# Turning the attention output of step 3 by transposing DMAs from SyncE in place of TensorE

## The chip, the cores and the metric

The kernel runs on one core of a Trainium2 chip. The metric is the time on the device in microseconds (us), lower is better. Executions of the kernel before on one chip agree here within about 1%. A granted TensorE clock of 1.00 is full speed: FFN matmuls of 384 columns then come every 0.163 us (kernel before, 16 of them from 50.08, clock 1.00 in the stretch 50 to 60).

## The reference, cut to what matters

```python
# attention, 4 batches x 8 heads x 768 positions x 64; five heads keep only 4 sink columns and a window of 64
scores = where(mask, q @ k.T / sqrt(64), -1e9)
a = softmax(scores)
attn = a @ v                                   # (B, H, S, D)
# FFN on the attention output, heads side by side: x is (3072, 512)
x = attn.transpose(0, 2, 1, 3).reshape(B * S, H * D)
h = max(x @ w1, x @ w2, x @ w3)                # (3072, 768)
out = h @ w_out                                # (3072, 512)
```

The kernel's FFN matmuls take x with its 512 features on the partitions (the tiles xT below), so each piece of attention output is turned first.

## The kernel before: the parts that matter

Work is cut into 16 steps t: four batches, two halves of 384 rows each, and in each half two quads of four heads. A step has two head pairs i, and each gives one tile x of 128 rows by 3 blocks of 128 columns. Two steps make the four tiles xT (hp = 0 to 3) that one half's FFN needs. Steps 0, 1 and 3 turn x on TensorE with a copy out of PSUM; the others do it by a transposing DMA from SyncE's queue:

```python
BY_DMA = (2, 4, 5, 6, 7, 8, 9, 10, 11, 12, 13, 14, 15)

def av(t, i):
    # ... value products into a PSUM bank o ...
    nc.vector.reciprocal(out=rc, in_=o[:, :, :, D])
    x = xp.tile([P, HB, 2, D], FP16, tag="x", name="x")
    nc.vector.tensor_tensor(out=x, in0=o[:, :, :, 0:D], in1=rc..., op=ALU.mult)     # cut
    if t in BY_DMA:
        nc.sync.dma_start(
            out=xT[b, half][hp], in_=x.rearrange("p a h d -> p (a h d)"), transpose=True
        )
    else:
        xs[t, i] = x

def turn_x(t, i, op=None):
    if t not in BY_DMA:
        # ... three TensorE transposes into tr, then one copy tr -> xT (VectorE for step 3) ...
    if hp == NHP - 1:
        queue.append(ffn(b, half))          # from here on this half's FFN is interleaved
```

The FFN's first product accumulates over the four tiles in turn, so the two tiles of step 3 are its third and fourth matmul:

```python
for ks in range(KS):
    nc.tensor.matmul(yy[:, 0:HALF], w_t[wi][:, ks, ...], xT[b, half][ks]..., start=(ks == 0), stop=(ks == KS - 1))
```

The softmax here doesn't subtract the row's maximum and nothing guards it: scores larger than these inputs give would overflow.

## Time and profile before

| | before |
|---|---|
| time, median | 200.65 us (200.58 to 200.71) |
| TensorE busy | 189.7 of 199.3 us, 95% |
| TensorE waits after 50.2 us | none |

In the list of waits a line reads: who waited on whose result, microseconds in total, how often, the longest. The kernel before:

```profile
PE tr L527 <- DVE x L505: 1.2, 3, 0.6
PE st L441 <- DVE KQ L190: 0.8, 2, 0.5
```

The first is the wait of the x transposes for VectorE, of which 0.64 us belongs to step 3. The second is that of step 4's scores for the turned keys, 0.53 us, directly behind step 3's transposes.

### The profile page before, as it was taken

To read this page: it belongs to the slowest core of one execution; us is meant where nothing else is said; L and a number is where in the kernel's file an instruction comes from. 1 tells how busy PE (TensorE), PEld (TensorE's weight loads), DVE (VectorE), ACT (ScalarE), POOL (GpSimd) and SP (SyncE) were. 2 spreads that over 40 slices of the span, in tenths; PEclk is the share of its full clock that TensorE was granted. 3 is DMA by queue.
4 is the path that set the end of the run, shared out by engine and by line. 5 is a ranking of instruction groups with operands and counts; after the bars stand their busy time and mean duration, and the time that the engine had idled before them with its cause. 6 is when DMAs were issued, how large, how long until landed. Compare 5 with 4: busy or idle time off the path is not lost.

```text
span 199.3 us, 5133 instructions
## 1 busy us (share of the span) xinstructions
PE 189.7 (95%) x2059; PEld 109.5 (55%) x2059; DVE 122.5 (61%) x241; ACT 131.7 (66%) x206; POOL 123.3 (62%) x154
## 2 busy tenths in 40 slices
PE   7897999996999999999999999999999999999992
PEld 2455555545566465574555565565555565755652
DVE  2698587999687829861555649961555234543540
ACT  4585798786966776676786775848758769323221
POOL 3599159789887906787969635799847447400000
PEclk9999999999999999999999999999999999999999
DMA  6999999994949991904359995513410250023004
GB/s 182 270 213 245 278 238 212 213 202 112 256 81 154 194 274 43 178 0 146 95 101 132 170 254 141 85 26 98 116 23 20 105 76 20 3 64 135 3 0 158
DMA packets 43245, 26.48 MB, mean 133 GB/s; under 512 B 33558, under 2 KB 38230, under 8 KB 43222
## 3 DMA queue, kind: packets, MB, share of 16 engines
q1 hardware_dynamic: 37206, 15.01, 34.9%
q0 software_dynamic: 4784, 10.23, 26.7%
q10 hardware_dynamic: 1232, 0.92, 1.5%
q8 instruction: 16, 0.26, 0.6%
q14 instruction: 7, 0.06, 0.1%
HBM read 25.17 MB, written 6.29 MB: 158 GB/s over the span
## 4 chain that ended last, share of the span: by engine, by line
PE 78%; DVE 8%; ACT 4%; DMA 3%; issue 3%; POOL 2%; SPq 1%; ACTq 0%; POOLq 0%; DVEq 0%
PE yy L338 43%; PE yy L364 12%; PE st L441 10%; PE oacc L495 8%; DVE KQ L190 4%; PE yst L338 3%; ACT pt L452 3%; DMA ks<-in_k_dram 2%; DVE x L505 2%; DMA out_dram<-ot 1%; PE tr L157 1%; PE yst L364 1%; POOL kn L139 1%; DVE hT L349 1%; POOL qn L139 0%
## 5 line engine op out<-in xcount | busy, mean ns | idle before, releaser
L479 POOL TENSOR_TENSOR pt<-pt,mk 128x512 f16<-128x512 f16 (+1 forms) x76 | 80.6, 1084 | 34.8 <-ACT pt L452 34.7
L452 ACT ACTIVATE pt<-st 128x1024 f16<-128x1024 f32 (+3 forms) x99 | 83.1, 894 | 19.4 <-PE st L441 18.6
L349 DVE TENSOR_TENSOR acc<-yy,acc 128x384 f16<-128x384 f32 x45 | 25.1, 558 | 28.9 <-PE yy L338 19.3
L338 PE MATMUL yy<-xT,w1t 128*128 128x384 f16 x180 | 36.1, 327 | 0.1
L338 PE MATMUL yy<-xT,w0t 128*128 128x384 f16 x180 | 35.6, 326 | 0.4 <-DVE xT L531 0.4
L338 PE MATMUL yy<-xT,w2t 128*128 128x384 f16 x180 | 35.7, 327 | 0.0
L346 ACT CAST acc<-yy 128x384 f16<-128x384 f32 x45 | 21.0, 485 | 17.0 <-PE yy L338 10.5
L364 PE MATMUL yy<-woutt,hT 128*128 128x512 f16 (+1 forms) x138 | 32.0, 375 | 0.0
L441 PE MATMUL st<-KQ 32*128 32x384 f16 (+4 forms) x560 | 28.7, 279 | 1.0 <-DVE KQ L190 0.8
L349 DVE TENSOR_TENSOR hT<-yy,acc 128x384 f16<-128x384 f32 x45 | 25.1, 560 | 6.6 <-PE yy L338 4.0
L495 PEld LDWEIGHTS <-pt 128*128 128x128 f16 x672 | 24.0, 97 | 5.3 <-issue 2.1
L190 DVE STREAM_TRANSPOSE KQ<-kq 128x384 f32<-128x384 f32 x24 | 25.7, 1130 | 0.0
L338 PEld LDWEIGHTS <-w0t 128*128 128x128 f16 x192 | 18.2, 98 | 12.9 <-issue 1.0
L495 PE MATMUL oacc<-va,pt 128*128 128x65 f16 x352 | 24.8, 193 | 0.3 <-ACT va L392 0.3
L338 PEld LDWEIGHTS <-w2t 128*128 128x128 f16 x192 | 17.6, 98 | 13.3 <-issue 2.1
L338 PEld LDWEIGHTS <-w1t 128*128 128x128 f16 x192 | 17.2, 98 | 12.8 <-issue 1.3
L370 ACT COPY ot<-yy 128x512 f32<-128x512 f32 x22 | 12.9, 588 | 15.9 <-PE yy L364 9.6
L364 PEld LDWEIGHTS <-hT 128*128 128x128 f16 x150 | 14.0, 98 | 14.6 <-issue 0.3
L441 PEld LDWEIGHTS <-KQ 32*128 32x128 f16 (+1 forms) x560 | 12.2, 93 | 17.8 <-issue 11.5
L495 PE MATMUL oacc<-vf,pt 128*128 128x65 f16 x320 | 21.2, 193 | 0.8 <-POOL vf L394 0.8
L505 DVE TENSOR_TENSOR x<-oacc,rc 128x384 f16<-128x384 f32 x32 | 17.8, 557 | 1.1
L503 DVE RECIPROCAL rc<-oacc 128x6 f32<-128x6 f32 x32 | 6.1, 192 | 20.0 <-PE oacc L495 19.8
(70 smaller groups left out, 129.9 us busy)
## 6 DMA issues: line engine op xcount, KB each, us to landing
out_dram<-ot SPq DMA_DIRECT2D x23, 256.0 KB, 3.1
vs<-in_v_dram SPq DMA_DIRECT2D x21, 256.0 KB, 6.3
kq<-in_k_dram POOLq DMA_DIRECT2D x6, 384.0 KB, 5.6
kq<-in_q_dram POOLq DMA_DIRECT2D x6, 384.0 KB, 8.0
qs<-in_q_dram ACTq DMA_DIRECT2D x4, 192.0 KB, 4.0
ks<-in_k_dram SPq DMA_DIRECT2D x4, 192.0 KB, 3.6
w0t<-in_moe_w_dram POOLq DMA_DIRECT2D x1, 768.0 KB, 7.4
ks<-in_k_dram POOLq DMA_DIRECT2D x2, 384.0 KB, 7.2
```

The costliest lines, as they stand in the source:

```text
L190: nc.vector.transpose(out=dst.rearrange("c (p j) -> c j p", j=n)[:, j0:j1], in_=src.rearrange("c (j i) -> c j i", i=R),)
L338: nc.tensor.matmul(yy[:, 0:HALF], w_t[wi][:, ks, ni * P : (ni + 1) * P], xT[b, half][ks].rearrange("p a t -> p (a t)"), start=(ks == 0), s ...
L346: nc.scalar.copy(out=acc[ni], in_=yy[:, 0:HALF])
L349: nc.vector.tensor_tensor(out=dst, in0=yy[:, 0:HALF], in1=acc[ni], op=ALU.max)
L364: nc.tensor.matmul(yo[:, 0:n], hT[ns][:, tb * P : (tb + 1) * P], woutt[:, ns, c : c + n], start=(ns == 0), stop=(ns == NNB - 1),)
L370: op(out=ot[:, c : c + n], in_=yo[:, 0:n])
L441: nc.tensor.matmul(sts[g // m][:, g % m, c0 : c0 + n * P], KQ[rows, 0, ki * P : (ki + 1) * P], KQ[rows, 1, t0 : t0 + n * P], start=(c0 == ...
L452: nc.scalar.activation(out=pts[t, i][:, u, h0 : h0 + m, 0:w], in_=st[:, :, 0:w], func=AF.Exp, scale=sc,)
L479: engine.tensor_tensor(out=x, in0=x, in1=m, op=ALU.mult)
L495: nc.tensor.matmul(o[:, qi, hl, 0 : D + 1], pt[:, u, hl, c : c + P], vv[:, 2 * hp + hl, ki, 0 : D + 1], start=(idx == 0), stop=(idx == len ...
L503: nc.vector.reciprocal(out=rc, in_=o[:, :, :, D])
L505: nc.vector.tensor_tensor(out=x, in0=o[:, :, :, 0:D], in1=rc.unsqueeze(3).to_broadcast([P, HB, 2, D]), op=ALU.mult,)
```

## The change

It is meant to take six more transposes from TensorE, the engine that bounds the kernel, and two copies from VectorE, since the other steps of the steady state do their turning by DMA already.

```diff
-    BY_DMA = (2, 4, 5, 6, 7, 8, 9, 10, 11, 12, 13, 14, 15)
+    BY_DMA = (2, 3, 4, 5, 6, 7, 8, 9, 10, 11, 12, 13, 14, 15)
```

## The prediction

> **What bounds the kernel now.** I read the busy line first, then TensorE's waits, then stretches of ten microseconds, and then the neighbourhood of step 3 in order of time, engine by engine and with SyncE's queue. The busy line, and three of the stretches (their columns: span, busy time and count of each engine, TensorE clock, DMA share, GB/s):
>
> ```profile
> PE 189.7 (95%) x2059; PEld 109.5 (55%) x2059; DVE 122.5 (61%) x241; ACT 131.7 (66%) x206; POOL 123.3 (62%) x154
> ```
> ```profile
> 40.00:50.00 10.00, 7.79 (x131) 4.52 (x127) 9.76 (x17) 7.53 (x12) 9.61 (x11) 1.00 0.70 155
> 50.00:60.00 10.00, 10.00 (x132) 6.07 (x121) 7.52 (x15) 8.01 (x14) 8.26 (x13) 1.00 0.80 171
> ...
> 180.00:190.00 10.00, 10.00 (x63) 6.00 (x62) 5.06 (x10) 2.98 (x6) 0.00 (x0) 1.00 0.14 54
> ```
>
> TensorE bounds it. From 50 us to 190 us each stretch but one is full (the other is 9.90 of 10), and the list of TensorE's waits, asked for 50.2 us to the end, is empty. Busy alone proves little, so I counted the work too. From the page's forms and from spacings read in this trace (a 384-column matmul every 0.163 us, one of 512 every 0.22, a score matmul every 0.035, an attention-value one every 0.032), seven FFN halves take 7x72x0.163 = 82 us and 7x18x0.22 = 28, twelve score steps some 480x0.035 = 17, 24 value products 504x0.032 = 16. That is about 143 us for a stretch of 140: there is no slack in which a delay after 50 us could be made good. Before 50 us there is some: in 40 to 50 TensorE is busy 7.79.
>
> Step 3 lies exactly at this border. TensorE in order of time (start, length, instruction, count, idle time before it):
>
> ```profile
> 47.43 0.41 PE L441 MATMUL st<-KQ 32*128 32x256 f16 x8
> 48.48 0.51 PE L527 MATMUL tr<-ident,x 128*128 128x128 f16 x6 [0.64 <-DVE x L505]
> 49.51 0.63 PE L441 MATMUL st<-KQ 32*128 32x384 f16 x16 [0.53 <-DVE KQ L190]
> 50.08 2.77 PE L338 MATMUL yy<-xT,w0t 128*128 128x384 f16 x16
> ```
> and VectorE beside it:
> ```profile
> 47.17 0.56 DVE L505 TENSOR_TENSOR x<-oacc,rc 128x384 f16<-128x384 f32 x1
> 47.86 0.56 DVE L505 TENSOR_TENSOR x<-oacc,rc 128x384 f16<-128x384 f32 x1
> 48.34 1.12 DVE L190 STREAM_TRANSPOSE KQ<-kq 128x384 f32<-128x384 f32 x1
> 49.25 0.65 DVE L531 COPY xT<-tr 128x384 f16<-128x384 f16 x2
> ```
>
> The two x tiles of step 3 are finished at 47.73 (pair 1) and 48.42 (pair 0). Six transposes and two copies have them turned by 49.90, and the first FFN product of this half starts at 50.08, the place where TensorE becomes saturated. The first accumulation needs all four xT tiles, those of step 3 as its third and fourth matmul.
>
> SyncE's queue at the same time:
>
> ```profile
> 46.46 0.52 SPq L371 DMA_DIRECT2D out_dram<-ot  x1
> 47.08 1.22 SPq L514 DMA_TRANSPOSE xT<-x  x1
> 48.39 2.14 SPq L208 DMA_DIRECT2D vs<-in_v_dram  x3
> 50.63 2.58 SPq L371 DMA_DIRECT2D out_dram<-ot  x2
> 54.54 10.21 SPq L514 DMA_TRANSPOSE xT<-x  x4
> ```
>
> The queue issues one thing after another with gaps of 0.1 us from 46.46 to 53.21. Then it is free for 1.3 us, and takes the first transpose of step 4 as soon as its x is there (54.52).
>
> [...] The trace agrees that they run: 26 of them, 2.3 us at the least from issue to landing.
> [...] the first one (issued at 42.94, behind three V loads) took 5.4 us instead of 2.4.
> [...] The trace shows the cold start though the granted clock reads 1.00 there:
>
> ```profile
> 1.26 4.45 PE L228 MATMUL st<-zero 128*128 128x512 f16 x10 [1.26 <-DVE warm L231]
> ...
> 40.55 1.47 PE L364 MATMUL yy<-woutt,hT 128*128 128x512 f16 x6
> ```
> Ten matmuls of 512 columns up to 5.64 are (5.64-1.26)/10 = 0.44 us apart; later six take 1.47 in all, about 0.22 apart. Triples of 128-column transposes are 0.32 us apart at 6.05 and 0.18 at 10.11. So it warmed between about 6.5 and 7.7, some 5.5 to 6.5 us after it began. No run shows yet what a gap in the middle does: the longest wait of TensorE in this trace is 1.3 us, at the start.
>
> **The change part by part.** The instruction order of both kernels shows these differences, and no others but buffer numbers: 6 transposes leave TensorE, 2 copies leave VectorE, SyncE's queue gets 2 transposing DMAs after the two output stores issued from 50.63, ahead of those of step 4. ScalarE and GpSimd are the same.
>
> *Removed.* The six transposes (0.51 us) and their wait (0.64) lie ahead of score matmuls that wait in any case for the KQ transpose on VectorE, which ends at 49.46. That one starts at 48.34, behind x, and is not moved. The copies (0.65 us) run beside it, and VectorE then idles 1.40 us before 51.30. The FFN product could start at most 0.1 us earlier. Gain: about 0 (TensorE would have to have no such wait for it to be 1).
>
> *Added.* Both x are ready at 48.42, but the queue comes to them only after the two stores, at 53.21. Issue of pair 1 at 53.3. A transpose's issue takes 1.19 us (the median of 26) and 0.1 us lies between issues, so pair 0 goes at 53.3 + 1.3 = 54.6. Landing: in 53 to 55 us the DMA view gives one of the stores and the transpose
>
> ```profile
> out_dram<-ot SPq DMA_DIRECT2D x1, 256.0 KB, 5.0
> xT<-x SPq DMA_TRANSPOSE x1, 2.4
> ```
> so the transpose issued at 54.54 in the kernel before landed in 2.4 us with the same stores ahead of it. Taking that for pair 0: 54.6 + 2.4 = 57.0. That of pair 1, issued earlier, is there by then.
>
> *Moved.* TensorE would do the first two FFN matmuls at 50.1 and stand at the third, which it began at about 50.08 + 2x0.163 = 50.4, until 57.0: a stall of **6.6 us**. [...] scores and value products of step 4 stand behind it. ScalarE, VectorE and GpSimd finish what they have and then idle. After it all the work from 50.4 us on follows unchanged, in a stretch without slack, so 6.6 us goes to the end.
>
> [...]
>
> Sum: 200.65 - 0 + 6.6 + 2.2 = **209.4 us**.
>
> **Rivals.** *The transposes are hidden, and six fewer on the bound engine is a gain.* For it: TensorE is at 95%, and 13 of 16 steps do it so already. Against it: those have several microseconds between x and the product that uses it, step 3 has 1.7 (48.42 to 50.08), less than even the 2.3 of the fastest landing, and the queue is not free for 4.8. It would give 200 to 200.7.
> *Stall without a cold clock.* [...] 207.2.
> *Slower landings.* Transposes that met loads from GpSimd's queue took far longer:
>
> ```profile
> xT<-x SPq DMA_TRANSPOSE x1, 6.9
> ```
> (issued at 58.26). Those loads were issued at 56.74 and 57.33, by a GpSimd that here will itself be waiting for TensorE, so I don't expect it. With 4 us more: 213 to 214.
> *Back-pressure at issue.* Issues can take 3.41 us with many small packets ahead, against 1.19. The small V packets are mostly gone by 53; if not, 1 to 2 us more: about 211.
> *The stall is partly given back.* DMA, VectorE and GpSimd get 6.6 us ahead; but TensorE waits for none of them after 50.2, so nothing can come back but tenths.
>
> **Range and chances.** The lower edge is the stall of some 6 us with hardly a penalty, 206.4; the upper edge full penalty with 1 us of slower issue or landing, 212.0. Faster by over 2% would need a mechanism that I see nowhere (1%); within 2% (under 204.7) needs a stall below 4 us, so a queue that reaches the transposes by about 51.5, or overtaking (4%); slower by over 2% the rest.
>
> **What would show it.** In TensorE's waits a new line: the FFN product on line 338 waiting for the transposing DMA, one time, 6 to 7 us, beginning near 50.4. SyncE's queue: stores until 53.2, then two transposes at 53.3 and 54.6, then step 4's after x, all later. The ten-microsecond stretch from 50 near 3.5 busy, those after full again. [...] The last output later by stall plus penalty. Wrong if the third matmul starts before 54 or after 60, if the spacing is 0.163 at once (then 207), or if TensorE shows new waits beyond 70 us from the shifted queue.

The forecast's sum came to 209.4 us, 200.65 - 0 + 6.6 + 2.2. The last term: 2.2 us for a TensorE that resumes at half speed after the stall. It stood as the estimate, since no run had yet shown a gap in the middle; the "full penalty" of the range belongs to it. What the runs show of the clock is below.

## More of the kernel before

A hand-made program gives the order of all engines. The rows around step 3 (first the FFN share, then whether the slot's scores are split in two, then what stands before the scores, after them, and at two later places of the slot):

```python
(2.2, True,  "turn 1 0 1 1, load_v 1 1", "", "v 3 1 pp, v 3 0 ap, x 2 0", "turn 1 1 0 0"),
(3.6, False, "turn 1 1 0 1", "x 2 1", "turn 1 1 1 1, av 3 1", ""),
(2.8, False, "v 4 0 pp, av 3 0", "turn 1 1 1 0", "v 4 1 ap", ""),
(3.6, False, "x 3 0, x 3 1", "", "", ""),
(3.6, False, "av 4 0", "", "x 4 0, v 5 1 pp", "x 4 1, v 5 0 ap"),
```

`load_v 1 1` is three DMAs of V from SyncE's queue, for the second half of batch 1, needed only by steps 6 and 7. The stores of finished FFN rows go to the same queue.

## The result, and the profile after

| | before | changed |
|---|---|---|
| time, median | 200.68 us | 209.48 us (209.14 to 210.01, 4 runs) |
| ratio | | 1.044 (95%: 1.042 to 1.047), slower |
| mean granted clock | 0.998 | 0.975 (one run 0.982) |

A ratio here is the mean time of one kernel's fast runs over that of the kernel before of the same rounds, so not quite the ratio of the medians.

The busy line of the changed kernel's page:

```profile
PE 190.7 (92%) x2053; PEld 109.5 (53%) x2053; DVE 122.4 (59%) x239; ACT 132.3 (64%) x206; POOL 123.1 (59%) x154
```

Six TensorE instructions fewer, and yet 1.0 us more busy time: some matmuls ran slower. The waits of TensorE:

```profile
PE yy L338 <- DMA xT<-x: 7.1, 1, 7.1
PE st L441 <- DVE KQ L190: 2.0, 2, 1.7
```

The new line at the top is the predicted one, an FFN product waiting for a transposing DMA once. The second grew from 0.8 us: what the transposes took (0.51, and 0.64 of waiting) has become waiting for the keys. In order of time, TensorE in the changed kernel:

```profile
47.56 0.41 PE L441 MATMUL st<-KQ 32*128 32x256 f16 x8
49.65 0.63 PE L441 MATMUL st<-KQ 32*128 32x384 f16 x16 [1.68 <-DVE KQ L190]
50.21 0.50 PE L338 MATMUL yy<-xT,w0t 128*128 128x384 f16 x2
57.78 3.94 PE L338 MATMUL yy<-xT,w0t 128*128 128x384 f16 x14 [7.07 <-DMA xT<-x]
```

Step 4's scores start at 49.65, against 49.51 before: nothing was gained there. The third FFN matmul was due at 50.21 + 2 x 0.163 = 50.54 and starts at 57.78. That is 7.24 us. The 14 matmuls behind the wait take 3.94 us. Before, they took the 2.77 us of all 16 less 2 x 0.163, or 2.44, so 1.50 us is lost here too. Together 8.74, against 1.0442 x 200.68 - 200.68 = 8.87 us of measured time.

Why the wait ends where it does is read from SyncE's queue (start, length of the issue, what, count):

```profile
48.64 2.16 SPq L208 DMA_DIRECT2D vs<-in_v_dram  x3
50.90 1.32 SPq L371 DMA_DIRECT2D out_dram<-ot  x2
52.31 2.17 SPq L514 DMA_TRANSPOSE xT<-x  x1
54.57 1.21 SPq L514 DMA_TRANSPOSE xT<-x  x1
```

The x tiles are ready at 47.86 and 48.55, but three loads and two stores are issued first. In the DMA view, where the last column is the time from issue to landing, the two transposes are these, first and second:

```profile
xT<-x SPq DMA_TRANSPOSE x1, 5.1
xT<-x SPq DMA_TRANSPOSE x1, 3.2
```

They land at 57.4 and 57.7, and TensorE goes on at 57.78. The slow matmuls are read in narrow stretches (columns as in the prediction; the third number from the right is the clock):

```profile
50.60:50.80 0.20, 0.11 (x1) 0.00 (x0) 0.00 (x0) 0.20 (x1) 0.20 (x2) 0.56 1.25 285
...
60.80:61.00 0.20, 0.20 (x3) 0.10 (x1) 0.00 (x0) 0.00 (x0) 0.00 (x0) 0.84 0.00 0
```

The clock falls to half (called cold below) just after 50.6 and is back just before 60.9. From 57.78 to 60.86 TensorE works at half speed, 3.08 us, and half of that, 1.54, is lost: the 1.50 above. And nothing comes back later: the stretches of ten microseconds from 60 to 200 are all full but one of 9.90, as those from 50 to 190 were before the change.

### The profile page after: what moved, and what is told of

It reads as the page before. It is cut to its first block, busy times and chain, and to the rows that moved or that the text cites. A ratio compares the mean times of both kernels' runs of the same rounds, so it can differ in the third digit from the quotient of the medians.

```text
span 208.0 us, 5125 instructions
## 1 busy us (share of the span) xinstructions
PE 190.7 (92%) x2053; PEld 109.5 (53%) x2053; DVE 122.4 (59%) x239; ACT 132.3 (64%) x206; POOL 123.1 (59%) x154
## 4 chain that ended last, share of the span: by engine, by line
PE 72%; DMA 9%; DVE 7%; POOL 3%; issue 3%; ACT 3%; SPq 1%; ACTq 0%; POOLq 0%; DVEq 0%
PE yy L338 40%; PE yy L364 11%; PE st L441 9%; PE oacc L495 8%; DMA w1t<-in_moe_w_dram 4%; DVE KQ L190 4%; PE yst L338 3%; DMA ks<-in_k_dram 2%; ACT pt L452 2%; DMA xT<-x 2%; DVE pt L479 1%; DVE x L505 1%; DMA out_dram<-ot 1%; PE yst L364 1%; POOL kn L139 0%
## 5 line engine op out<-in xcount | busy, mean ns | idle before, releaser
L338 PE MATMUL yy<-xT,w0t 128*128 128x384 f16 x180 | 37.2, 336 | 7.5 <-DMA xT<-x 7.1
```

What stands on the lines that cost most here:

```text
L338: nc.tensor.matmul(yy[:, 0:HALF], w_t[wi][:, ks, ni * P : (ni + 1) * P], xT[b, half][ks].rearrange("p a t -> p (a t)"), start=(ks == 0), s ...
```

## The experiments

**Theory A.** The transposes stand in SyncE's queue behind loads and stores; they land 7 us after TensorE wants them; TensorE has no slack behind that point, so all of it reaches the end, and the clock that falls meanwhile takes 1.5 to 2.5 us on top. **Rivals:** B, a transposing DMA is simply slow here, wherever it stands; C, the time comes from another effect of the change (banks, buffers); D, the clock plays no part. The kernel before gave 201.1 to 201.2 us (200.2 to 202.4).

### Does a delay here reach the end? (e2_pad_before)

The kernel before, with zero matmuls for a delay:

```diff
+    def busy_work(n):
+        sink = bank([P, 512], FP32, "yy")
+        for _ in range(n):
+            nc.tensor.matmul(sink, zero[:, 0:P], zero, start=True, stop=True)
-        (3.6, False, "x 3 0, x 3 1", "", "", ""),
+        (3.6, False, "x 3 0, x 3 1", "busy 31", "", ""),
```

> The kernel before (transposes on TensorE) with the same 31 matmuls of zeros between step 4's first scores and the FFN product, 31 x 0.218 = 6.8 us of delay for TensorE and nothing else. If no slack follows, as theory A says, all of it reaches the end: 200.7 + 6.8 = 207.4. If later slack gives some of a delay back, 204 to 206, and then the stall explains less of the 8.8 us than it seems.

Measured: 207.93 us, ratio 1.0345 (1.029 to 1.040), so 6.9 us for 6.8 us of inserted work. There is no slack; a delay of TensorE at this place is paid in full. The kernel's own tuning had left no later wait into which it could vanish.

### What does the clock cost? (e1_busy_stall, then e12_busy_again beside e11_changed_again)

The changed kernel with the same zero matmuls ahead of the stalled product:

```diff
-        (3.6, False, "x 3 0, x 3 1", "", "", ""),
+        (3.6, False, "x 3 0, x 3 1, busy 6", "busy 31", "", ""),
```

> The changed kernel with matmuls of zeros put in front of the stalled FFN product (6 ahead of step 4's first scores, 31 of 512 columns behind them, about 1.3 and 6.8 us), so that TensorE is busy while the transposes are on their way; same results. Theory A with a cold clock: the transposes land as before near 57.7, but the clock reads 1.00 throughout and the first 14 FFN matmuls take about 2.45 us in place of 3.94, so 1.5 us less: 208.0. Without a part played by the clock: 209.5 or slightly more.

Measured: 207.86 us, ratio 1.033 (1.027 to 1.038), clock 1.00. TensorE in order of time:

```profile
50.34 6.86 PE L486 MATMUL yy<-zero 128*128 128x512 f16 x31
57.04 0.49 PE L338 MATMUL yy<-xT,w0t 128*128 128x384 f16 x2
57.83 2.44 PE L338 MATMUL yy<-xT,w0t 128*128 128x384 f16 x14 [0.30 <-DMA xT<-x]
```

The 14 matmuls begin at 57.83, practically as in the changed kernel (57.78), and take 2.44 us in place of 3.94. By the ratios, 1.033 against 1.044, useless work made the kernel faster. They were run at other times.

> The changed kernel itself once more, beside the next run and on the same chip, so that the two can be compared directly: 1.044 of the kernel before, a TensorE wait of about 7 us for the transposing DMA, a cold clock for 6.8 or 10.2 us.

> The kernel of e1_busy_stall again, beside the changed one. If the clock is what the matmuls of zeros change, it takes 1.5 to 2.5 us less than the changed kernel of this call (half of the resumed work done at half speed), with a granted clock of 1.00; if chips or rounds made the difference, the two lie within 0.7 us.

Measured: the changed kernel 208.39 us, ratio 1.038 (1.029 to 1.046), its TensorE wait 6.0 us, cold for 10.24 us; with the zero matmuls 207.33, ratio 1.031 (1.026 to 1.036). By the means of four runs each (208.73 and 207.37) 1.4 us, a little under the 1.5 that I had set as the least; the intervals overlap, so this pair alone does not show a gain. In that profile the 37 zero matmuls lasted longer than the stall would have, so the difference understates the clock. Rival D falls by the 14 matmuls; the size is better shown by the next pair but one.

### The place in the queue (e3_loads_behind, e4_first_in_queue)

```diff
-  "turn 1 0 1 1, load_v 1 1"
+  "turn 1 0 1 1"
-  "v 4 0 pp, av 3 0"
+  "v 4 0 pp, av 3 0, load_v 1 1"            # e3
+  "v 4 0 pp, av 3 0, send, load_v 1 1"      # e4: the two stores are held back and sent here
```

> The changed kernel with the three V loads of the next batch's second half issued behind step 3's two transposes; the two output stores stay ahead of them. Theory A (place in SyncE's queue): the queue reaches the transposes at about 49.7 and 51.0 us in place of 52.3 and 54.6, they land near 53.3 (2.4 us, something more behind the stores), TensorE's wait falls from 7.1 to about 3 us; with the cold clock still there 205 us, without it 203.5. Rival B (such a transpose takes some 3 to 5 us here by itself, because the DMA engines are busy): the wait falls by the earlier issue alone but the landing stays over 3 us, 206 or more. Rival C (the time comes from something else that the change does, the order of banks or buffers): no change, 209.5.

Measured: 206.44 us (204.5 to 207.2), ratio 1.025 (1.018 to 1.032), which leaves open whether it is over 2%. TensorE's wait, and the matmuls behind it:

```profile
PE yy L338 <- DMA xT<-x: 2.7, 1, 2.7
```
```profile
52.23 4.03 PE L338 MATMUL yy<-xT,w0t 128*128 128x384 f16 x14 [2.67 <-DMA xT<-x]
```

The wait fell from 7.1 to 2.7 us as theory A said; the time stands 1.4 us over its figure with the cold clock. The profiled run (204.53) had the clock down for 3.4 us, mean 0.991; the other three read 0.983, so about twice that, and were 1.2 to 2.7 us longer.

> As the run before, and the two output stores too are issued behind the transposes, so these stand directly behind step 2's second one. Theory A: issue at about 48.6 and 49.8 us, landing at 51 to 52.2, TensorE waits about 1 us or a little more, 201 to 202 us, within 1% of the kernel before. Rival B: landing after 3 us or more, wait 2.5 us and over, 203.5. Rival C: 209.5.

Measured: 206.09 us, ratio 1.025 (1.020 to 1.030). My figure of 201 to 202 was a miss. The wait and the chain of work that ended last, then TensorE:

```profile
PE yy L338 <- DMA xT<-x: 2.3, 1, 2.3
```
```profile
48.50 3.82 DMA xT<-x
```
```profile
52.36 4.64 PE L338 MATMUL yy<-xT,w0t 128*128 128x384 f16 x14 [2.30 <-DMA xT<-x]
```

Two things went otherwise. The second transpose, issued at 48.50 directly behind the first with nothing else ahead of both but step 2's, took 3.8 us to land, not 2.4; so rival B has a part. It is not the pair as such: in the kernel before, the two issued directly behind one another at 88.64 and 89.94 took 2.3 us each. The DMA view of e4 from 50.2 to 50.6 shows what was under way beside it:

```profile
q8 instruction: 1, 0.02, 14.7%
```

That is one packet of 16 KB on a queue that the profile calls instruction, 0.94 us long (14.7% of 16 engines over 0.4 us). One was under way beside the late second transposes of e3 and e9 too. By my count over all 13 traces, the 99 transposes of known landing that met next to no other packets took 2.28 to 2.43 us, seconds of pairs included; the nine that met a packet of a queue of that name and next to nothing else took 2.6 to 3.3 (3.3 at 174.86 in the kernel before, beside one of 8 KB). The two go together in the traces; no experiment tested it, and it does not account for all of the 3.8 us.
Besides, with x ready at 47.90 and 2.3 us to land, even an empty queue does not deliver by 49.89, when the third matmul was due. And the clock fell at 50.5, though the wait is only 2.3 us, and came back at 57.33. So 4.97 us of resumed work ran at half speed, which costs 2.5 us: as much as the stall itself (52.36 - 49.89 = 2.47). The sum, 4.96 us, is the measured 2.47% of 201.2.

### The same with a busy TensorE (e9_front_busy)

e4 with `busy 6` ahead of step 4's scores and `busy 10` behind them.

> The run e4_first_in_queue with matmuls of zeros ahead of (6) and behind (10 of 512 columns) step 4's first scores, so that TensorE is not idle while it waits for the two transposes; same results. If the cold clock takes more than the stall there, as its trace suggests (14 FFN matmuls in 4.64 us in place of 2.45, and the value products behind them slow too; 5.2 us of resumed work at half speed, so 2.6 us), then this runs at a clock of 1.00 and 203.3 to 203.7 us, 2.3 to 2.6 less than e4. If the clock plays no part: as e4, 206.

Measured: 203.32 us, ratio 1.0125 (1.008 to 1.017), clock 1.00, 2.8 us less than e4.

```profile
52.18 2.44 PE L338 MATMUL yy<-xT,w0t 128*128 128x384 f16 x14 [0.18 <-DMA xT<-x]
```

What is left, 2.5 us, is the lateness of the transpose alone: without the 10 matmuls the third FFN matmul was due at 49.34 + 0.33, and it starts at 52.18. This settles the clock's part: the same lateness costs 5.0 us with an idle TensorE and 2.5 us with a busy one.

### One pair only: at the front, and in its place (e10_front_one_pair, e6_one_pair_in_place)

```diff
-        if t in BY_DMA:
+        if t in BY_DMA and (t, i) != (3, 0):
-        if t not in BY_DMA:
+        if t not in BY_DMA or (t, i) == (3, 0):
```

e10 has this on top of e4, e6 on top of the changed kernel. Both keep pair 0 on TensorE and turn pair 1, ready 0.7 us earlier, by DMA.

> As e4_first_in_queue, but only pair 1 of step 3, whose x is ready 0.7 us earlier, goes by a transposing DMA; pair 0 stays on TensorE. Issue at about 47.3, landing by 49.8 to 50.3 (2.4 to 3 us), against 50.4 when the FFN product wants it: hidden, so the time of the kernel before within 0.5 us (201), no cold clock, and no gain either, because the three transposes saved stand before a wait for VectorE's KQ transpose. If a DMA on this path costs more than its latency, 202 or more; if transposes saved on TensorE were worth their time, 200.5 or less.

Measured: 200.98 us against 201.11, ratio 0.999 (0.995 to 1.003). The transpose is hidden:

```profile
49.70 0.63 PE L449 MATMUL st<-KQ 32*128 32x384 f16 x16 [0.69 <-DVE KQ L190]
50.27 2.77 PE L338 MATMUL yy<-xT,w0t 128*128 128x384 f16 x16
```

All 16 matmuls run through. Three transposes fewer on TensorE bring nothing: the wait for the keys before the scores is 0.69 us here, 0.53 in the kernel before and 1.68 with all six gone.

> The changed kernel with pair 0 back on TensorE and only pair 1 on a transposing DMA, with loads and stores left ahead of it in the queue: the twin of e10_front_one_pair but for the place. If the place is what costs, the one transpose lands about as late as the two did (issued near 52.3, landing 55.5 to 57), TensorE waits 5 to 7 us, 207 to 209.5 us. If the second transpose behind the first was the trouble, it lands by 53 and the time is 203 to 204.5.

Measured: 208.27 us, ratio 1.036 (1.031 to 1.040).

```profile
PE yy L338 <- DMA xT<-x: 5.1, 1, 5.1
```

The same single transpose, the same arithmetic; only the three loads and two stores stand ahead of it. It was issued at 50.07 and took 5.2 us. By the ratios (two chips) e10 and e6 differ by 7 us, and the place in the queue is all that was changed: 5.1 us is the stall, and some 2.4 the clock, cold from 53.30 to 60.13 while TensorE resumed at 55.26. Rival C falls with this: e3 and e4 too moved only the issues of loads and stores, and got to 1.025 where C had forecast no change.

### The loads from another queue (e7_loads_by_gpsimd)

```diff
+            int(b), int(h), (nc.gpsimd,) * HB if (b, h) == ("1", "1") else None
```

> The changed kernel with the three V loads in question issued from GpSimd's queue, so they no longer stand ahead of the transposes in SyncE's ring [...]. If the place in the ring is all: as e3_loads_behind, TensorE waits about 3 us, 205 to 206.5. If the load on the engines counts as well: transposes issued near 50 land only after 5 us or more (as those of step 4 did beside GpSimd's loads in the kernel before), a wait of 5 to 7 us, 208 to 209.5.

Measured: 207.36 us, ratio 1.032 (1.027 to 1.037). This run is confounded, as a look at its waits shows:

```profile
PE oacc L495 <- POOL vf L394: 3.1, 1, 3.1
PE yy L338 <- DMA xT<-x: 0.6, 1, 0.6
```

GpSimd, busy with masks, now issues the loads ahead of a V tile that TensorE needs, and TensorE waits 3.1 us for that instead (0.7 in the changed kernel), goes cold at 47.0, warms, and goes cold again at 53.8. Step 3's transposes, issued at 49.99 and 51.53, landed in 3.9 and 2.7 us, but by then the loads of the other queue were done (their last packet ended at 50.19), so the second reading was not tested on them. Step 2's two, under way together with those loads, took 8.8 and 5.7 us, against 5.5 and 2.3 in the changed kernel, which fits the second reading. It is no way out.

### Other work in the gap (e8_ffn_later)

```diff
-        (3.6, False, "x 3 0, x 3 1", "", "", ""),
+        (3.6, False, "", "", "", ""),
         # one row later unchanged, then in the row after it:
-        (2.8, False, "", "", "av 4 1", "av 5 0, load 2 0, v 6 0 pp"),
+        (2.8, False, "", "x 3 0, x 3 1", "av 4 1", "av 5 0, load 2 0, v 6 0 pp"),
```

> The changed kernel with the FFN of this half begun two slots later, so that step 4's value products and scores (about 2 us of TensorE's work in 8 matmul groups) are done while the transposes are on their way. Theory A: the wait before the FFN shrinks by about 2 to 3 us, and TensorE is not idle for so long at a stretch, so 205 to 207.5 us. If TensorE's slack further on paid for the stall, or if scores ahead of time only made it wait for ScalarE later: no gain, 209.5 or more.

Measured: 206.46 us (205.2 to 207.9), ratio 1.025 (1.018 to 1.032): 2 to 4 us less than the changed kernel, by the ratios 1.025 against 1.038 (e11, whose interval overlaps) to 1.044. No line for the transposing DMA is left among TensorE's waits, but the attention work brought forward waits for ScalarE and GpSimd in turn and runs on a cold clock:

```profile
54.34 1.53 PE L441 MATMUL st<-KQ 32*128 32x384 f16 x16 [0.68 <-ACT pt L452]
```

(16 such matmuls take 0.63 us warm.) The clock was down for 10.2 us here. The gap is partly filled, not closed.

No run beats the kernel before. The best variant, e10, equals it.

## Why the prediction was right

209.4 was predicted, 209.48 measured. Step by step:

- **TensorE bounds, and has no slack after 50 us:** right. e2 shows it directly, 6.9 us of time for 6.8 us of delay.
- **Nothing is gained by the removal:** right. The wait for the keys grew from 0.53 to 1.68 us, by just what the transposes and their own wait had taken; e10 shows the same with three transposes fewer and no stall.
- **The transposes wait for their turn in SyncE's queue:** right. e10 against e6 (201.0 and 208.3 us), and e3, show it. In its detail the step was off in ways that partly cancelled. The queue came to the first transpose at 52.31, not 53.3, since the stores issued faster. The issue of the first took 2.17 us and not 1.19, so the second went out at 54.57 (54.6 predicted). That one then took 3.2 us, not 2.4: landing 57.7 and not 57.0. The step "taking that for pair 0: 2.4 us" is the mis-sized term.
- **Stall 6.6 us:** 7.24 in the profile, and a shorter wait, 6.0 in place of 7.1 us, in e11's profile of the same kernel.
- **Clock 2.2 us:** right that TensorE resumes at half speed (granted clock 0.50 from 57.78 to 60.86), wrong on when the clock falls, and 1.50 in size. The estimate had it fall well into the gap. In fact it fell at 50.62, about as the stall began. In the 3.41 us up to then, the length of the shortest cold stretch found, TensorE was busy for 1.73 us; the 1.68 us wait for the keys, opened by the removal, lay in them. How much of the resumed work is slow differs between two profiles of this kernel: 3.08 us here, 4.03 in e11 (56.21 to 60.24).
- The cold stretches found lasted 3.41 (e3, and two in e7), 6.83 (e4, e6) and 10.24 us (changed, e8, e11), within 0.01 us one, two and three times 3.41, with edges at other times in each run.
- The rival of a back-pressure at issue was partly there (an issue of 2.17 us in place of 1.19); slow landings through GpSimd's loads and a gain given back later were not. Against hidden transposes the prediction set 1.7 us between x and its use; to the third matmul, the first that needs step 3's tiles, it is 2.0 (48.42 to 50.41), still less than the 2.3 of the quickest landing.

The sum came out within 0.1 us because a stall of 0.6 us too little and a clock penalty of 0.7 us too much met. The stall and the slow clock are shown; the closeness of the number is luck.

What stays open: whether the instruction packets, which go with the late landings in e3 and e4, cause them, and what lets the clock fall.

## What to carry to other kernels

Before work is moved from a busy engine to a DMA, read two things: how soon the result is wanted after it can be sent, and what the issuing queue has in front of it at that moment; steps of the same kind elsewhere in the kernel do not tell. Work taken from ahead of another wait was worth nothing here, even on the engine that bounds. And a stall of TensorE is to be counted with the clock: 2.5 us of late data cost 5.0 us here (e4), and half of it could be had back by matmuls of zeros (2.5 us in e9).

## What the runs show of the clock and of transposing DMAs

- In the 3.41 us before the clock fell in the middle of a run TensorE was busy for 1.73 (changed, e11), 1.70 (e8), 1.67 and 0.70 (e7, second and first time), 1.28 (e4), 0.87 (e3) and 0.31 us (e6), so in none of these was it idle throughout. After 3.41 us with 1.74 us busy (e3, to 48.69) and 2.09 (e6, to 49.89) the clock stayed up. But busy time, as the profile models it, does not tell when the clock falls: after 3.41 us with 1.52 us busy (e1, from 201.58) and 1.62 us (e2, from 200.24), both at the end of the run, it stayed up too.
- In e4 the clock fell at 50.50, 0.4 us into the second gap, and the longest gap in the 3.41 us up to then was 1.7 us; it stayed down for 6.83 us and cost 2.5 us.
- A single transpose, measured here for fp16 tiles of 128 x 384: 1.2 us of the queue for an issue with nothing ahead (1.19, the median of 26 in the kernel before); 2.3 to 2.4 us from issue to landing with next to no other traffic, also directly behind another (2.3 each at 88.64 and 89.94); 2.6 to 3.3 beside a packet of a queue called instruction (3.0 in e3); for the first one behind loads or stores of the same queue 5.4 (before, step 2), 5.5 and 5.1 (changed, steps 2 and 3), 5.2 (e6), and 4.0 behind stores alone (e3).
- What stands ahead in the queue: the same single transpose with three loads and two stores ahead (e6, 208.27 us) and without them (e10, 200.98 us) differ by 7 us of run time, the cold clock included.
